# Decay attention and a sticky mixture of experts: batch 0's queries and keys turned by TensorE, its loads reordered, gates that count their transfer, a two-column minimum in one view, and less room for four ranked experts

## The chip, the cores and the metric

The kernel runs on one core of a Trainium2 chip. The metric is the device time in microseconds, as the median of several executions. Fewer is better.

## The reference

```python
scores = scale * q @ k^T                           # 8 batches, 8 heads, 576 positions, head size 64, scale 1/8
cum    = cumsum(log(clip(f, 1e-4, 1)))
attn   = softmax(causal(scores + cum[:, None] - cum[None, :]))
x      = (attn @ v) as [8, 576, 512]               # the heads side by side
logits = x @ w_gate; local = sigmoid(x @ w_local)  # 8 experts
for each batch, for s in order:                    # the routing is sticky
    e = argmax(logits[s]) if s == 0 or local[s] < 0.5 else prev_e
    out[s] = softmax(logits[s])[e] * (relu(x[s] @ w1[e]) @ w2[e])   # w1 512x1024, w2 1024x512
```

The inputs are fp32 and drawn at random.

## The kernel before

**Attention, batch by batch.** fp32 values are split into a high and a low fp16 part. For every batch the queries and keys are turned so that head size lies on partitions: tile A holds high and low parts on 128 partitions, tile B (`QB`, `KB`) the high part on 64 partitions and six rows more that carry the decay. A score is two products, A by A and B by B. A batch has 25 units: for each pair of heads a c, two a, a b and a c unit, then four d units for the last 64 positions and one more. Each unit passes through stages: scores on TensorE (`sc`, L868), row maximum on VectorE (`mx`, L879), exponential on ScalarE (`ex`, L899), the transposition of the weights on TensorE (`tr`, L914), the split on ScalarE and VectorE (`hi`, L919, `lo`, L923), the product with v on TensorE (`av`, L893), and the division by the sum (L954, L958). In d units the maximum is the smaller of two negated maxima (`mn`, L986).

**What sets the order.** The engines' queues are written by hand. A planner (`issue`, `start_of`, `step`) keeps a clock for each engine with estimated costs, and issues next the stage that could start first, with weights. A list `DUE` of times on that clock triggers groups of moves (`moves`, lists `ORD0`, `ORDA`, `ORDB`): loads, splits on GpSimd, turning. All transfers but indirect ones stand in the SyncE queue, which issues strictly in order and waits at each until its source is ready and its destination free. From batch 2 on, queries and keys are turned in groups of eight blocks by TensorE (`prep_turned`, `group`, stages `tq` and `eq`); a `needs` entry keeps scores behind them. From batch 1 on, the load buffer of one batch is refilled with the next one's as soon as it has been split.

**Batch 0, before.** `start` lets ScalarE (`high`) and GpSimd and VectorE (`low`) split queries and keys of heads 0 to 3 into fp16. TensorE turns these heads (`turn_high`, L552, `turn_first`, L546), adds the decay rows by a small product (`add_decay`, L557), and ScalarE and VectorE copy the results out of PSUM (`untwist`). Heads 4 to 7 and the last positions are turned by transfers (`turn`, `turn_last`) and copied by more transfers. The values are split by ScalarE and VectorE for heads 0 to 5 (`due_v`, `split_v`). The decay's parts for the last 64 positions, `spt`, are made on VectorE (`parts`, L247 and L251) in `start`.

**Gate and routing.** When a batch's attention is done, its rows are split on GpSimd and turned by three transfers (`finish_main`, `finish_last`). A side chain then runs the gate (`mult`, L816) of that batch on TensorE, with a routing step (`route`) for every second batch. `side_next` tells when the next piece of the chain may run: before, a gate may be issued once its three transfers have been issued.

**Experts.** The first two experts have fixed places, the other six are sorted by their number of tokens. Each rank has room for a fixed number of tokens (`CAP2`, `RANK2`, in units of 64). `experts` computes z = x w1 (L1690, 192 products of half the room's columns, or 96 of all of them up to 512) and y = h w2 (L1712, 24 products of 512 columns for every 128 tokens; a last 64 tokens take 48 products of 256 columns, L1716). Tokens above the room go to a loop at the end, one round of 128 tokens each, which does not run when there are none.

```python
after.append(ends[dep])                          # start_of: a stage waits for the one before it
if due and due[0][0] <= t and all(room[r] for r in due[0][2]):
    due.popleft()[1]()                           # issue: moves that have come due go first
```

## Time and profile before

| | |
|---|---|
| median of 3 runs | 856.01 us (855.11 to 859.09) |
| the profiled execution, its own time | 858.83 us |
| its span, first to last instruction | 857.1 us |
| TensorE busy | 785.4 us, 92% |
| VectorE, ScalarE, GpSimd busy | 529.3, 434.4, 408.9 us |
| granted TensorE clock, mean | 0.976 |
| moved by DMA | 122.46 MB, 143 GB/s |

The span minus the busy time of the engine that bounds is what waits cost at most. Attention ends at about 440 us; the experts fill the rest. Rows of merged instructions give one start and the whole length, and a product's length contains its passage through the array, so the rate of a stream of products is read from starts.

### The profile page before, as it was taken

To read this page: it belongs to the slowest core of one execution; us is meant where nothing else is said; L and a number is where in the kernel's file an instruction comes from. 1 tells how busy PE (TensorE), PEld (TensorE's weight loads), DVE (VectorE), ACT (ScalarE), POOL (GpSimd) and SP (SyncE) were. 2 spreads that over 40 slices of the span, in tenths; PEclk is the share of its full clock that TensorE was granted. 3 is DMA by queue.
4 is the path that set the end of the run, shared out by engine and by line. 5 is a ranking of instruction groups with operands and counts; after the bars stand their busy time and mean duration, and the time that the engine had idled before them with its cause. 6 is when DMAs were issued, how large, how long until landed. Compare 5 with 4: busy or idle time off the path is not lost. (4 is left out here: it accounts for less than half of the span.)

```text
span 857.1 us, 21126 instructions
## 1 busy us (share of the span) xinstructions
PE 785.4 (92%) x8510; PEld 546.9 (64%) x8510; DVE 529.3 (62%) x1125; ACT 434.4 (51%) x807; POOL 408.9 (48%) x479
## 2 busy tenths in 40 slices
PE   5897999889998799878987899999999999999996
PEld 3676778767877678767753555575564847566543
DVE  8885878898867888798848742443163644525120
ACT  4785878758866688657821413333242423324221
POOL 9598938488753968532976252221311212130201
PEclk9998999999989999998999999999999999999999
DMA  7979768596781859329674641848264553736101
GB/s 167 192 165 193 160 112 168 123 180 144 140 197 42 157 140 158 70 47 229 161 165 185 194 142 50 216 147 203 95 171 149 155 182 121 193 116 185 51 0 47
DMA packets 196517, 122.46 MB, mean 143 GB/s; under 512 B 136220, under 2 KB 172318, under 8 KB 196396
## 3 DMA queue, kind: packets, MB, share of 16 engines
q1 hardware_dynamic: 190273, 101.68, 51.6%
...
## 5 line engine op out<-in xcount | busy, mean ns | idle before, releaser
L1690 PE MATMUL z<-xT,wh 128*128 128x288 f16 (+4 forms) x960 | 182.3, 301 | 3.8 <-DVE hl L1671 3.8
L899 ACT ACTIVATE P<-st,nm 128x512 f32<-128x512 f32 (+3 forms) x288 | 152.4, 584 | 38.5 <-DVE nm L879 35.3
L879 DVE TENSOR_REDUCE nm<-st 128x1 f32<-128x512 f32 (+4 forms) x264 | 134.1, 542 | 23.2 <-PE st L875 16.8
L1671 DVE SCALAR_TENSOR_TENSOR hl<-z,hh 128x576 f16<-128x576 f32 (+5 forms) x80 | 53.0, 662 | 154.0 <-ACT hh L1670 153.8
L919 ACT CAST ph<-pt 128x512 f16<-128x512 f32 (+1 forms) x200 | 115.8, 583 | 50.1 <-PE pt L914 48.6
L914 PE MATMUL pt<-ident,P 128*128 128x128 f32 x784 | 124.7, 283 | 13.0 <-DVE pl L923 8.0
L923 DVE TENSOR_TENSOR pl<-pt,ph 128x512 f16<-128x512 f32 x168 | 111.6, 668 | 26.3 <-ACT ph L919 24.0
L1690 PEld LDWEIGHTS <-wh 128*128 128x128 f16 x960 | 93.2, 98 | 43.7 <-issue 4.9
L1690 PE MATMUL z<-xT,wl 128*128 128x288 f16 (+4 forms) x480 | 118.4, 301 | 0.0
L1712 PE MATMUL y<-uh,hh 128*128 128x512 f16 x288 | 109.9, 381 | 1.6 <-ACT o L1680 1.6
L1712 PE MATMUL y<-uh,hl 128*128 128x512 f16 x288 | 109.9, 382 | 0.0
L1712 PE MATMUL y<-ul,hh 128*128 128x512 f16 x288 | 109.7, 381 | 0.0
L1670 ACT ACTIVATE hh<-z 128x576 f16<-128x576 f32 (+5 forms) x80 | 46.0, 575 | 121.1 <-PE z L1690 121.0
L914 PEld LDWEIGHTS pt<-ident,P 128*128 128x128 f32 x784 | 85.8, 144 | 28.9 <-issue 7.5
L1712 PEld LDWEIGHTS <-hh 128*128 128x128 f16 x576 | 56.5, 98 | 70.4 <-issue 6.2
L1682 POOL DMA_INDIRECT out_dram<-o,ranki x26 | 27.3, 1051 | 149.0 <-ACT o L1680 115.8
L893 PE MATMUL xp<-VH,pl 128*128 128x65 f16 (+1 forms) x960 | 92.3, 195 | 4.3 <-DVE pl L923 4.3
L893 PE MATMUL xp<-VH,ph 128*128 128x65 f16 (+1 forms) x960 | 94.3, 198 | 0.9 <-ACT ph L919 0.9
L893 PE MATMUL xp<-VL,ph 128*128 128x65 f16 (+1 forms) x960 | 93.2, 196 | 0.0
L893 PEld LDWEIGHTS <-ph 128*128 128x128 f16 (+1 forms) x1920 | 85.0, 103 | 7.7 <-issue 2.5
L868 PE MATMUL st<-KB,QB 70*128 70x256 f16 (+4 forms) x448 | 80.1, 287 | 8.5 <-DMA KB<-Ak 7.1
L868 PE MATMUL st<-Ak,Aq 128*128 128x256 f16 (+4 forms) x448 | 80.7, 291 | 7.3 <-ACT P L899 7.1
...
## 6 DMA issues: line engine op xcount, KB each, us to landing
...
```

Of the source, the lines that this page charges most:

```text
L868: nc.tensor.matmul(st[p0:p0 + m, co:co + n], lhsT=queries(lq, kk, h, c), rhs=rhs, start=(ps == 0 and first and co == col), stop=(ps == 1), ...
L879: nc.vector.tensor_reduce(dst, src, axis=AX.X, op=ALU.max, negate=True)
L893: nc.tensor.matmul(xo, lhsT=a[:, c0:c0 + m], rhs=w[:, vi, :], start=False, stop=(i == n - 1 and jj == 2), skip_group_check=True)
L899: nc.scalar.activation(P[:, c0:c1].rearrange("p (k x r) -> p k r x", r=2, x=64), st[:, c0:c1].rearrange("p (k r x) -> p k r x", r=2, x=64) ...
L914: nc.tensor.matmul(U["pt"][:, i * 128:(i + 1) * 128], lhsT=P[:, i * 128:(i + 1) * 128], rhs=ident, is_transpose=True, start=(i == 0), stop ...
L919: nc.scalar.copy(U["ph"][:, :cols], U["pt"][:, :cols])
L923: nc.vector.tensor_tensor(U["pl"][:, :cols], U["pt"][:, :cols], U["ph"][:, :cols], ALU.subtract)
L1670: nc.scalar.activation(hv, z[:, 0:nh, 0:wd], AF.Relu)
L1671: nc.vector.scalar_tensor_tensor(lv, z[:, 0:nh, 0:wd], 0.0, hv, ALU.max, ALU.subtract)
L1682: nc.gpsimd.indirect_dma_start(out=outf, out_offset=bass.IndirectOffsetOnAxis(ap=scat(t), axis=0), in_=o, in_offset=None, bounds_check=NT ...
L1690: nc.tensor.matmul(z[:, a, 0:wd], lhsT=w[:, d, fc * 128:(fc + 1) * 128], rhs=xT[:, x, a * wd:(a + 1) * wd], start=(i == 0), stop=(i == len ...
L1712: nc.tensor.matmul(y, lhsT=a[:, fc, t * 128:(t + 1) * 128], rhs=u[:, fc], start=(i == 0), stop=(i == len(prods) - 1))
```

## The change

Experts' rooms are now given in tokens: 608, 608, 576, 576, 544 and 480 for the six ranks, where they were 640, 640, 576, 576, 576 and 512. The two fixed experts keep 640 and 704. Parts of tiles of 96 and 32 tokens take the place of whole and half tiles.

In batch 0, TensorE transposes fp32 queries and keys of heads 0 to 3 as they were loaded (`turn_head`), ScalarE takes the high part out of PSUM and a second time with the decay rows (`head_hi`, `head_b`), and VectorE the low part (`head_lo`). Heads 0 and 1 are turned ahead of the decay, head 2 right behind it, head 3 as a planned stage (`head_3`). Heads 4 to 7 and the last positions become planned groups like those of later batches (`group`, `first_turns`), and the transposing transfers of batch 0 are gone. GpSimd no longer scales queries, splits the values of heads 2 to 7, and makes `spt` (`last_parts`). Fills of `QB` and `spk` go from GpSimd to ScalarE and VectorE. `ORD0` is now three lists at three due times; the loads of batch 2's queries and keys leave `ORDB` and get due times of their own (`ORDC`). A gate's start on the planner's clock has to lie 4500 ns behind the estimated end of its batch's last split (`XR`, `XL`). `mn` is a reduction over two columns of one strided view. Batch 0's units 10 to 24 get `needs`.

```diff
-CAP2 = (10, 11)
-RANK2 = (10, 10, 9, 9, 9, 8)
+CAPC = (640, 704)
+RANKC = (608, 608, 576, 576, 544, 480)
...
-ORD0 = moves_of("q:l :k2 q:t4 k:l q:p k:t4 q0:m :sv k:p q:c k:c q1:m q:t k:t :lm q:M k:m :at 0:R 1:R :lv")
+ORD0 = moves_of("k:A q:A q:l k:l :k2 :sv q:p k:p")
+ORD1 = moves_of('q0:m q1:m')
+ORD2 = moves_of(':lm q:M k:m k:M :sp :at 0:R 1:R :lv q:a k:a')
...
-DUE = (("k2", 11000), ("q2", 12500), ("k3", 14500), ("q3", 15500), ("v", 18000), ("v4", 20500), ("a", 26000), ("b", 29000))
+XL = 4500
+LATE = ((12500, 'kh'), (13500, 'qh'), (15500, 'q2'), (15500, 'q3'), (17500, 'k2'), (17500, 'k3'), (22000, 'q4'), (23000, 'k4'))
+DUE = (('k2', 11500), ('q2', 12300), ('0', 12500), ('1', 20600), ('2', 25000), ('a', 27000), ('b', 29000), ('c0', 47000), ('c1', 56000))
...
-    for c in range(2):
-        nc.gpsimd.memset(QB[0][64:70, 16 * c + 8:16 * c + 16], -1.0)
...
+    spk = cp.tile([97, 512], F16, name="spk")
+    nc.vector.memset(spk, 0.0)
+    nc.vector.memset(spk[96:97], 1.0)
     nc.vector.memset(KB[0][64:70, 16:32], 1.0)
-
-    spk = cp.tile([97, 512], F16, name="spk")
-    nc.gpsimd.memset(spk, 0.0)
-    nc.gpsimd.memset(spk[96:97], 1.0)
+    for c in range(2):
+        nc.scalar.activation(flat(QB[0][64:70, 16 * c + 8:16 * c + 16]), ident[64:70, 0:1].broadcast_to([6, 1024]), AF.Copy,
+                             scale=0.0, bias=-1.0)
...
+    for t, x in (pick[:, 0, :, 3:6], 1.0 / SCALE), (pick[:, 1, :, 0:3], 1.0):
+        nc.gpsimd.affine_select(out=t, in_=t, pattern=[[-1, 4], [-32, 3]], compare_op=ALU.not_equal, fill=x, base=0,
...
+    def group(b, nm, j):
...
+        def tq():
+            t16 = Tq[b][nm + "t"]
+            U["pt"] = psS.tile([128, 8, 128], F16, name="st")
+            for a in range(4 if j == 4 else 8):
+                nc.tensor.transpose(U["pt"][:, a], t16[:, 8 * j + a], ident16)
...
+        return {"key": (b, nm, j), "tq": ("PE", 460 * c, tq, {"psS": 1}, {}), "eq": (eng, cost, eq, {}, {"psS": 1})}
...
+    def last_parts():
+        x = cu[:, 512:576]
+        for j in range(3):
+            nc.gpsimd.tensor_scalar(spt[:, j], x, 1.0, 1.0, ALU.mult, ALU.mult)
+            if j < 2:
+                nc.gpsimd.tensor_tensor(x, x, spt[:, j], ALU.subtract)
...
+    def turn_head(h, nm):
+
+        st = psX.tile([128, 512], F32, name="xp") if h == 2 else psS.tile([128, 512], F32, name="st")
         for a in range(4):
-            nc.tensor.transpose(pt[:, a], Tq[0][nm + "t"][:, 4 * h + a], ident16)
-        return pt
-
-    def turn_high(h, nm):
-        st, c0 = psS.tile([128, 512], F32, name="st"), 64 * (nm == "k")
-        for a in range(4):
-            nc.tensor.matmul(st[0:64, 128 * a:128 * a + 128], lhsT=Tq[0][nm + "t"][:, 4 * h + a, c0:c0 + 64], rhs=ident16,
+            nc.tensor.matmul(st[0:64, 128 * a:128 * a + 128], lhsT=LT[0, nm][:, 4 * h + a], rhs=ident, is_transpose=True,
                              start=(a == 0), stop=True, skip_group_check=True)
         return st
...
+    def head_hi(st, h, nm):
+        nc.scalar.activation(of_head(Tq[0][nm + "A"], TOP if nm == "q" else LOW, h, nm), of_bank(st, 64, nm), AF.Copy,
+                             scale=SCALE if nm == "q" else 1.0)
+
+    def head_b(st, h, nm):
+        nc.scalar.activation(of_head(Tq[0][nm + "B"], slice(0, 70), h, nm), of_bank(st, 70, nm), AF.Copy,
+                             scale=SCALE if nm == "q" else 1.0)
+
+    def head_lo(st, h, nm):
+        A = Tq[0][nm + "A"]
+        hi = of_head(A, TOP if nm == "q" else LOW, h, nm)
+        if nm == "q":
+            for c in range(2):
+                dst, src, top = (x[:, :, c] for x in (of_head(A, LOW, h, nm), of_bank(st, 64, nm), hi))
+                nc.vector.scalar_tensor_tensor(dst, src, SCALE, top, ALU.mult, ALU.subtract)
         else:
-            copy(by_head(dst, n, h), pt[0:n].rearrange("p (a c x) -> p a c x", a=4, c=2) if len(pt.shape) == 2 else
-                 pt.rearrange("p a (c x) -> p a c x", c=2))
+            nc.vector.tensor_tensor(of_head(A, TOP, h, nm), of_bank(st, 64, nm), hi, ALU.subtract)
...
-        high("q", 0, 2, True)
-        high("k", 0, 2)
-        high("k", 2, 4)
-        high("q", 2, 4)
         other_masks()
-        for h in range(2):
-            low("q", h, h + 1, nc.gpsimd, True)
-            low("k", h, h + 1, nc.gpsimd)
-        low("k", 2, 4, nc.gpsimd)
+        for C in range(2):
+            load_main(0, "q", C, 4, 8)
         load_v(0, groups=((0, 2),), last=False)
+        for C in range(2):
+            load_main(0, "k", C, 4, 8)
         by_chunks()
         parts(spm, lg[:, 0:512], 1, True)
-        for C in range(2):
-            load_main(0, "q", C, 4, 8)
         put_aug()
-        heads(0)
-        low("q", 2, 4, nc.vector)
-        heads(1)
-        parts(spt, cu[:, 512:576], 0)
-        split_v(0, 2, True)
-        for C in range(2):
-            load_main(0, "k", C, 4, 8)
+        for h in range(2):
+            heads(h)
+            for nm in "kq":
+                head_hi(HS[h, nm], h, nm)
+        decays(0)
+        decays(1)
+        heads(2)
+        decays(2)
+        for h in range(2):
+            for nm in "kq":
+                head_b(HS[h, nm], h, nm)
+                head_lo(HS[h, nm], h, nm)
         load_v(0, groups=((2, 8),), last=False)
-        for nm in "kq":
-            aug_main(0, nm, 4)
-
-        for nm in "qk":
-            for x in pieces(nm, 4, 8):
-                x()
+        vh, vl, v0 = parts_v(0, 2)
+        nc.scalar.copy(vh, v0)
+        for x in pieces("q", 4, 8):
+            x()
+        nc.gpsimd.tensor_tensor(vl, v0, vh, ALU.subtract)
+        for x in pieces("k", 4, 8):
+            x()
+        split_v(2, 4)
+
+    def due_0():
         for nm in "qk":
             LT[1, nm] = LT[0, nm]
             new_prep(1, nm)
         for x in ORD0:
+            moves(x)
+
+    def due_1():
+        assert all(n > -9 or u['key'][2] > 1 for n, u, _ in line['tq'])
+        for x in ORD1:
+            moves(x)
+
+    def due_2():
+        for x in ORD2:
...
+    def due_head(nm):
+        head_hi(HS[2, nm], 2, nm)
+        head_b(HS[2, nm], 2, nm)
+        head_lo(HS[2, nm], 2, nm)
+        clock["ACT"] += 960
+        clock["DVE"] = max(clock["DVE"] + 640, clock["ACT"] + 800)
+
+    def head_3(nm):
+        U = {}
+
+        def tq():
+            U["st"] = turn_head(3, nm)
+            add_decay(U["st"], 3, nm)
+
+        def eq():
+            for f in head_hi, head_b, head_lo:
+                f(U["st"], 3, nm)
+            clock["DVE"] = max(clock["DVE"], clock["ACT"] + 1100) + 640
+
+        return {"key": (0, nm, -1), "tq": ("PE", 500, tq, {"psS": 1}, {}), "eq": ("ACT", 960, eq, {}, {"psS": 1})}
+
+    def first_turns():
+        for t, x in LATE:
+            u = head_3(x[0]) if x[1] == "h" else group(0, x[0], int(x[1]))
+            u["ready"] = t
+            n = count[0] * 1e-4 - 10
+            count[0] += 1
+            for st, prev in ("tq", None), ("eq", "tq"):
+                line[st].append((n, u, prev))
...
+            XR[b] = max(clock["POOL"], clock["PE"]) + XL
...
-                nc.vector.tensor_tensor(nm[:, c:c + 1], nm[:, 44:45], nm[:, 40 + j:41 + j], ALU.min)
+                nc.vector.tensor_reduce(nm[:, c:c + 1], nm[:, 40 + j:45:4 - j], axis=AX.X, op=ALU.min)
...
-        for i, u in enumerate(units if b > 1 else ()):
-            u["needs"] = [(b, x, min(i // 10 * 2 + 1, 4) if i < 20 else 4) for x in "qk"]
+        for i, u in enumerate(units):
+            u["needs"] = [(b, x, min(i // 10 * 2 + 1, 4) if i < 20 else 4) for x in "qk"] if b > 1 or b == 0 and i > 9 else ()
...
-    clock = {"PE": T0, "ACT": T0, "DVE": T0, "POOL": T0}
+    clock = {"PE": T0, "ACT": T0 + 900, "DVE": T0 + 1300, "POOL": T0}
...
+        if hasattr(chain[0], "batch") and side["run"] is None:
+            after.append((XR[chain[0].batch], "PE"))
...
-        nt = 128 * n + (64 if half else 0)
+        n, mh = (nt // 128, nt % 128) if half else ((nt + 127) // 128, 0)
...
+                    m = min(128, nt - 128 * t)
+                    nc.tensor.matmul(y[0:m], lhsT=a[:, fc, t * 128:t * 128 + m], rhs=u[:, fc], start=(i == 0),
...
+                        nc.tensor.matmul(y[mh * r:mh * r + mh, 0:DM // 2], lhsT=a[:, fc, t * 128:t * 128 + mh],
```

**SyncE queue, batch 1's turned queries and keys against batch 2's loads** (ldq and ldk are the load buffers of queries and keys, Aq, Ak, QB and KB the tiles A and B). Before:

```order
L182 DMA ldv<-in_v_dram 128x8x64
L185 DMA ldv<-in_v_dram 64x4x64 x2
L162 DMA ldq<-in_q_dram 128x8x128 x2
L169 DMA ldq<-in_q_dram 64x4x64 x2
L162 DMA ldk<-in_k_dram 128x8x128 x2
L169 DMA ldk<-in_k_dram 64x4x64 x2
L378 DMA QB_121<-Aq 64x2x1024 x2
L382 DMA QB_121<-Aq 64x512
L375 DMA KB_123<-Ak 64x2048 x2
L382 DMA KB_123<-Ak 64x512
```

Now:

```order
L182 DMA ldv<-in_v_dram 128x8x64 x2
L185 DMA ldv<-in_v_dram 64x4x64 x2
L362 DMA QB_109<-Aq 64x2x1024 x2
L366 DMA QB_109<-Aq 64x512
L162 DMA ldq<-in_q_dram 128x8x128 x2
L169 DMA ldq<-in_q_dram 64x4x64 x2
L359 DMA KB_111<-Ak 64x2048 x2
L366 DMA KB_111<-Ak 64x512
L162 DMA ldk<-in_k_dram 128x8x128 x2
L169 DMA ldk<-in_k_dram 64x4x64 x2
```

Each pair of copies of batch 1 now stands ahead of batch 2's load of the same tensor; before, both loads stood ahead of all copies.

**SyncE queue, the late tokens of batch 3** (xl, turned into xlt for the gate; xr are the other tokens). Before:

```order
L341 DMA QB_121<-augm 3x32x64 x2
L351 DMA QB_121<-augt 3x512
L757 DMA xs<-xr 64x4x1024 x2
L378 DMA QB_121<-Aq 64x2x1024 x2
L382 DMA QB_121<-Aq 64x512
L339 DMA KB_123<-augm 3x4096
L351 DMA KB_123<-augt 3x512
L781 DMA_TRANSPOSE xlt<-xl 128x4x128
L787 DMA xs<-xl 128x1x256 x2
```

Now:

```order
L343 DMA QB_109<-augm 3x32x64 x2
L353 DMA QB_109<-augt 3x512
L732 DMA xs<-xr 64x4x1024 x2
L756 DMA_TRANSPOSE xlt<-xl 128x4x128
L763 DMA xs<-xl 128x1x256 x2
L362 DMA QB_109<-Aq 64x2x1024 x2
L366 DMA QB_109<-Aq 64x512
```

The transfer that turns xl stood behind the copies of batch 4's queries, and stands ahead of them now.

**VectorE at the start of batch 7** (HI, RH and LO are the marks of a routing step, nm the row maxima, pl the low parts of the weights). Before:

```order
L1473 TENSOR_TENSOR hm<-t_192,ov 128x10
L1479 TENSOR_TENSOR HI<-imain,hm 128x480
L1483 TENSOR_SCALAR RH<-HI,irow 128x10x48
L1485 TENSOR_SCALAR RH<-HI,irow 128x2x48
L1490 TENSOR_TENSOR RH<-HI,icol 128x10x48
L1491 TENSOR_TENSOR LO<-i_176,lo 128x1280
L879 TENSOR_REDUCE nm<-st 128x1 x5
L879 TENSOR_REDUCE nm<-st 128x2
L879 TENSOR_REDUCE nm<-st 128x1
L1501 TENSOR_TENSOR invi<-st,invi 128x96
```

Now:

```order
L1451 TENSOR_TENSOR hm<-t_188,ov 128x10
L855 TENSOR_REDUCE nm<-st 128x1 x2
L1457 TENSOR_TENSOR HI<-imain,hm 128x480
L855 TENSOR_REDUCE nm<-st 128x2
L1461 TENSOR_SCALAR RH<-HI,irow 128x10x48
L899 TENSOR_TENSOR pl<-pt,ph 128x512
L1463 TENSOR_SCALAR RH<-HI,irow 128x2x48
L855 TENSOR_REDUCE nm<-st 128x1
L1468 TENSOR_TENSOR RH<-HI,icol 128x10x48
L1469 TENSOR_TENSOR LO<-i_172,lo 128x1280
L930 RECIPROCAL rs<-xp 128x4
L899 TENSOR_TENSOR pl<-pt,ph 128x512
```

The five marks stood together ahead of the maxima, and are now spread between maxima and splits.

## Rows read from the trace of the kernel before

**Rows 1.** Busy time in stretches of the span: the stretch and its length, then for PE, PEld, DVE, ACT and POOL the busy microseconds (and the instructions), PEclk (the TensorE clock that was granted: 1.00 is 2.4 GHz, 0.50 is 1.2 GHz), the share of the DMA engines, and GB/s.
```profile
72.00:76.00 4.00, 1.20 (x7) 0.83 (x7) 0.47 (x1) 0.00 (x0) 3.92 (x5) 0.58 1.18 165
76.00:80.00 4.00, 4.00 (x68) 3.33 (x66) 2.42 (x6) 2.44 (x5) 1.97 (x2) 0.57 0.84 60
...
248.00:252.00 4.00, 4.00 (x24) 2.80 (x23) 1.74 (x6) 2.33 (x4) 0.00 (x0) 0.50 0.93 252
...
352.00:356.00 4.00, 4.00 (x33) 2.91 (x32) 3.09 (x10) 2.00 (x5) 3.71 (x6) 0.57 0.08 18
...
388.00:392.00 4.00, 4.00 (x23) 3.00 (x23) 2.60 (x5) 2.40 (x6) 0.00 (x0) 0.50 1.09 255
392.00:396.00 4.00, 4.00 (x45) 2.98 (x43) 3.26 (x12) 2.81 (x6) 0.74 (x1) 0.81 0.96 311
680.00:700.00 20.00, 19.85 (x124) 11.75 (x122) 12.63 (x17) 7.23 (x10) 4.36 (x3) 1.00 0.75 205
```

**Rows 2.** Timeline of TensorE in the first microseconds: start, length, engine, line and operation, out<-in, shapes, and how many instructions were merged into the row; in brackets the idle time ahead of it and what ended that.
```profile
12.13 1.01 PE L557 MATMUL st<-spk,pick 97*6 97x512 f16 x2 [0.74 <-DVE spk L246]
...
15.98 0.61 PE L868 MATMUL st<-Ak,Aq 128*128 128x512 f16 x1
...
16.91 0.63 PE L868 MATMUL st<-Ak,Aq 128*128 128x128 f16 x3
...
17.98 0.41 PE L868 MATMUL st<-Ak,Aq 128*128 128x128 f16 x3
...
24.28 0.38 PE L546 MATMUL pt<-ident,t16k 128*128 128x128 f16 x4 [2.17 <-DVE Ak L561]
...
26.93 1.06 PE L914 MATMUL pt<-ident,P 128*128 128x128 f32 x4
```

**Rows 3.** Timeline of VectorE there, same columns. L247 and L251 make the fp16 parts of the decay (spm the first 512 positions, spt the last 64), L879 is a row maximum.
```profile
9.10 0.42 DVE L247 CAST spm<-lg 64x512 f16<-64x512 f32 x1
...
15.48 1.05 DVE L247 CAST spt<-cu 64x64 f16<-64x64 f32 x1
...
16.82 2.00 DVE L247 CAST spt<-cu 64x64 f16<-64x64 f32 x1
...
19.88 3.14 DVE L247 CAST spt<-cu 64x64 f16<-64x64 f32 x1
...
22.56 1.34 DVE L879 TENSOR_REDUCE nm<-st 128x1 f32<-128x512 f32 x3
```

**Rows 4.** Timeline of ScalarE there, same columns: the logarithm, the table load for the exponential, one head's copy out of PSUM, the first exponential.
```profile
5.01 0.68 ACT L229 ACTIVATE lg<-ft 64x576 f32<-64x576 f32 x1 [2.93 <-DVE ft L228]
5.71 1.28 ACT L230 ACT_TABLE_LOAD   x1
...
12.75 0.58 ACT L561 CAST KB<-st 70x512 f16<-70x512 f32 x1 [2.81 <-PE st L557]
...
23.27 0.71 ACT L899 ACTIVATE P<-st,nm 128x512 f32<-128x512 f32 x1 [1.90 <-DVE nm L879]
```

**Rows 5.** Timeline of GpSimd: the first split of batch 1's queries.
```profile
38.67 1.05 POOL L310 TENSOR_SCALAR t16q<-ldq 128x1024 f16<-128x1024 f32 x1 [6.08 <-DMA ldq<-in_q_dram]
```

**Rows 6.** Timeline of the SyncE queue; a length here is the time to issue, x the number of transfers. The first load of batch 2 (three more like it follow), and the copies of batch 1's key halves.
```profile
56.62 1.59 SPq L162 DMA_DIRECT2D ldq<-in_q_dram  x2
...
66.67 2.68 SPq L375 DMA_DIRECT2D KB<-Ak  x2
```

**Rows 7.** Timeline of TensorE where batch 1 begins.
```profile
69.89 0.38 PE L868 MATMUL st<-Ak,Aq 128*128 128x512 f16 x1
74.80 0.59 PE L868 MATMUL st<-KB,QB 70*128 70x512 f16 x1 [4.53 <-DMA KB<-Ak]
```

**Rows 8.** Timeline of GpSimd in the gate of batch 3: the last split of its late tokens (xl).
```profile
237.41 0.67 POOL L314 TENSOR_TENSOR xl<-xnl,xl 128x256 f16<-128x256 f32 x1
```

**Rows 9.** Timeline of the SyncE queue there: batch 4's copies of query halves, then the transfer that turns xl.
```profile
239.91 1.76 SPq L378 DMA_DIRECT2D QB<-Aq  x2
...
243.77 1.83 SPq L781 DMA_TRANSPOSE xlt<-xl  x1
```

**Rows 10.** Timeline of TensorE there.
```profile
246.74 0.59 PE L816 MATMUL st<-wg,xlt 128*64 128x18 f16 x8 [1.94 <-DMA xlt<-xl]
```

**Rows 11.** Who TensorE waited for, over the whole span: line, microseconds in total, times, longest.
```profile
PE st L816 <- DMA xlt<-xl: 4.4, 2, 2.4
...
PE st L868 <- DMA KB<-augt: 1.4, 1, 1.4
```

**Rows 12.** Timeline of VectorE as batch 7 begins: the first of five marks of a routing step, and the row maxima behind them.
```profile
380.89 1.46 DVE L1479 TENSOR_TENSOR HI<-imain,hm 128x480 f16<-128x480 f16 x1
...
386.45 3.32 DVE L879 TENSOR_REDUCE nm<-st 128x1 f32<-128x512 f32 x7
```

**Rows 13.** Timeline of TensorE there.
```profile
387.92 0.59 PE L868 MATMUL st<-Ak,Aq 128*128 128x512 f16 x1 [4.66 <-ACT P L899]
```

**Rows 14.** Timeline of TensorE in the experts: two products that follow each other.
```profile
452.37 0.38 PE L1712 MATMUL y<-uh,hh 128*128 128x512 f16 x1
452.58 0.38 PE L1712 MATMUL y<-ul,hh 128*128 128x512 f16 x1
```

**Rows 15.** VectorE's groups by shape: count, busy microseconds, mean ns, idle time ahead.
```profile
L986 DVE TENSOR_TENSOR nm<-nm 128x1 f32<-128x1 f32 x32 | 8.6, 269 | 1.0
...
L954 DVE RECIPROCAL rs<-xp 128x2 f32<-128x2 f32 x32 | 5.1, 160 | 2.6 <-PE xp L893 1.9
```

More of the change, by code (lines that the diff above doesn't have):

```diff
@@ L693, in due_b @@
     def due_b():
+        assert all(n > -9 for n, u, _ in line['tq'])
         for x in ORDB:
@@ L696, in due_b, with due_c @@
         open_small()
+        EX["run"] = True
+    def due_c(i):
+        for x in ORDC[i]:
+            moves(x)
     def pieces(nm, h0, h1):
@@ L730, in split_v, with decays @@
-    def split_v(h0, h1, fast=False):
-        tv = [x.rearrange("p (c h) d -> p c h d", c=4) for x in (VH[0][:, 0:32], VL[0][:, 0:32], LT[0, "v"][:, 0:32])]
-        split(tv[0][:, :, h0:h1, 0:64], tv[1][:, :, h0:h1, 0:64], tv[2][:, :, h0:h1], fast)
-    def due_v(h0, h1):
-        split_v(h0, h1, True)
-        clock["ACT"] += 480
-        clock["DVE"] += 600
-    XT, XD = {}, {}
+        for nm in "kq":
+            HS[h, nm] = turn_head(h, nm)
+    def decays(h):
+        for nm in "kq":
+            add_decay(HS[h, nm], h, nm)
@@ L1636, in early_weights, with tokens @@
         return out
-    def tokens(pool, xT, cols, n, rows=NT, half=False):
-        for i in range(n + half):
-            m = 128 if i < n else 64
+    def tokens(pool, xT, cols, n, rows=NT):
+        for i in range((n + 127) // 128):
+            m = min(128, n - 128 * i)
             xg = pool.tile([128, 2 * DM], F16, name="xg", bufs=3)
@@ L1773 @@
                 init_gate()
-            if not due:
+            if "run" in EX:
                 if b < B - 1 or i < XP:
```

291 lines of the change are left out of this document (104 added, 187 removed).

## The prediction

> **What bounds the kernel now.** The windows come first: in the experts TensorE is busy 19.85 of 20 us at full clock [rows 1], so time is saved there only by giving it fewer columns. Attention is different. It ends at about 440 us, and TensorE waits in a few places for a transfer or an exponential; after such a wait the granted clock was 0.50 to 0.58, that is 1.2 GHz for all or most of 4 us, with TensorE busy all or most of them [rows 1], so a wait costs its length and about 2 us more. The timelines of the engines, TensorE first and then the one that it waited for, give the places; the list of waits gives the totals. The profiled execution took 858.83 us, 2.8 above the median of 856.01, and the sum is made against it. A measurement of this kernel can tell 0.5%, 4.3 us, from no change.
>
> **a. Batch 0's start.** Before, the two decay products run at 12.13 and the first score at 15.98 [rows 2]. Its maximum comes only at 22.56 [rows 3] and the exponential at 23.27 [rows 4]: ahead of it VectorE makes `spt`, three casts of 64 columns that take 1.05, 2.00 and 3.14 us, where a cast of 512 columns took 0.42 [rows 3]. TensorE waits 2.17 us and transposes the first weights at 26.93 [rows 2].
>
> Now ScalarE first fills `QB` (two instructions; with the table load of 1.28 [rows 4] that is 3.3 us by a length of 1.0 each, my choice between the 0.58 of a copy [rows 4] and the 1.76 us of VectorE's fill of twice the columns that falls away, so 1 is near the middle), against 2.93 us that it was idle ahead of the logarithm [rows 4]: the decays come 0.4 later. TensorE then runs four decays ahead of the scores, and head 2's eight transposes. Two decays took 1.01 with their passage through the array, so four take about 1.7; four fp32 transposes took 1.06 [rows 2], so head 2's eight about 1.7. With 0.9 for ScalarE's copies, which the scores wait for, the first score starts at 12.5 + 1.7 + 1.7 + 0.9 = 16.8, 0.8 later. But `spt` is on GpSimd and not in front of the maxima: with maximum and exponential following as they did ahead of the transposes, those stand at 20 to 21.7 instead of 26.93, with one more unit scored by then (0.5). Still to be done after that are head 3 (1.3) and the 40 transposes of the groups, 2.2 at 0.054 each (128 columns at the rate in f). Net: 26.93 - 21.7 + 0.5 - 1.3 - 2.2 = 1.25 with the late end and 2.95 with the early one; the 1.0 us in which ScalarE waited [rows 4] for copies that now need no VectorE adds up to 1.0 to both. I take **-3.1** of 1.25 to 3.95, near the top, since no `spt` is left ahead of the first maximum. ScalarE gets about 3.1 us more of copies there, at nothing, beside its idle 2.81 and 1.90 [rows 4]; without that cover they cost 3.1. GpSimd waits 6.08 us for batch 1's load [rows 5], so its `spt` and splits have room; if it is late, groups q4 and k4 are, by about 1 us.
>
> The new transposes weigh on the clock. The same three score products took 0.63 at 16.91 and 0.41 at 17.98 [rows 2]: the clock rose from half to full while TensorE did transposes, decays and scores in turn. The Trainium skill, "TensorE: Matmul & The Clock Gate", section "Part 4: PE-mode transpose", says that full clock does not engage for transpose mode, which is not counted as busy in the same way. By it the start gives +0.9 and not -3.1. Of what TensorE did ahead of the rise only a part were transposes, so the trace does not refute it; it is rival C.
>
> **b. Batch 1's halves.** The queue issues batch 2's load at 56.62, waits for its buffer, and reaches the copy of key halves at 66.67 [rows 6]. TensorE does the first product at 69.89 and waits 4.53 us for that copy [rows 7]; the clock is 0.58 and 0.57 behind it [rows 1], and 0.43 of the 5.2 us up to 80 is 2.2 lost. Now both copies stand ahead of the loads they waited behind. The load itself leaves later, at due times of its own, and has 50 us until batch 2. I take **-6.8** of 0 to -6.8.
>
> **c. The gates.** GpSimd has split the late tokens at 238.1 [rows 8], but the transfer that turns them goes out at 243.77 [rows 9], behind batch 4's copies. The gate waits 1.94 [rows 10]; two gates wait 4.4 in all [rows 11], with the clock at 0.50 and 0.57 behind them [rows 1]: 2.0 + 1.7. Now the transfer stands ahead of these copies, and the gate is planned 4500 ns behind the split. Behind a waiting gate stood scores, and behind SyncE's transfer batch 4's halves, which go 1.8 later but are not yet needed. **-8.1** of 0 to -8.1.
>
> **d. The last decay rows of batch 0** stood behind batch 1's in SyncE's queue, and are put ahead of them (ORD2). The wait for KB<-augt, 1.4 [rows 11], goes: **-1.4**; late next would be KB's last copy, which stands directly behind.
>
> **e. Marks of a routing step.** VectorE does five of them in one go from 380.89, maxima pile up to seven at 386.45 [rows 12], and TensorE waits 4.66 for an exponential [rows 13]; the clock is 0.50, then 0.81 [rows 1], 2.0 + 0.8 more: 7.5. Now maxima stand between the marks. But no rule makes it so; it fell out of a plan that differs from batch 0 on. Half: **-3.7** of 0 to -7.5.
>
> **f. The experts' rooms.** z takes 192 products of half the room: 16 columns fewer for 608 against 640, twice, 2 x 3072; 544 against 576 is the same 3072; 480 against 512 is 96 products by 32 columns, 3072. y keeps its columns: a part tile of 96 tokens still moves 512, one of 32 still 48 times 256. Products follow each other 0.21 us per 512 columns [rows 14], 0.42 ns each: 12288 columns are **-5.2**, the surest term, since nothing else bounds there.
>
> **g. The minimum.** 32 of them took 269 ns; the nearest row of an instruction on two columns is the reciprocal, 160 ns [rows 15]. 0 to -3.5; only d units wait for it, and I take **-1.0**. The Trainium skill, "VectorE: DVE Perf Modes", section "Rules for kernel authors", speaks against it: it calls a reduction the slowest operation of VectorE. By it this term would be 0 or a small plus; no row of before has a reduction of two columns.
>
> **h. The other plan.** Every stage from batch 0 on is issued in another order. A new wait can cost from 0 to what the largest cost here, 7.5. The trace has five large ones in eight batches, of which I have taken four to go and one half; one that comes back nearly whole is likely: **+6**, between 0 and 15 (two whole ones).
>
> Sum: -3.1 - 6.8 - 8.1 - 1.4 - 3.7 - 5.2 - 1.0 + 6 = -23.3, so 835.5 on this execution and about **835** for the median.
>
> **Rivals.** A: the plan gives back all that c and e save, 11.8 in place of h's 6. For: nothing in the list of moves fixes where marks fall. Against: the order of the two excerpts of SyncE's queue is fixed. 835 + 5.8 = 841. Chance 0.21.
> B: the change does not do what it says in batch 1: the copies stand ahead of the loads, but their source, the turned groups, is planned as late as before. +6.8: 842. Chance 0.08.
> C: the fp32 transposes leave the clock at half through batch 0. Two stretches of 4 us, as 76 to 80 [rows 1], cost 2 each: the start gives +0.9 and not -3.1, 839. For: these scores begin at half clock. Against: they show it rise [rows 2]. Chance 0.12. The section of the Trainium skill named in a has it so.
> D: slower. A rank's tokens are more than its smaller room, and the loop at the end runs. One round loads an expert's weights, 4.19 MB, at 205 GB/s [rows 1] 20.5 us, and does 96 products of 128 columns and 24 of 512, 5.2 + 5.2: 31 us on 835, at least 866. It decides from one token above the room. Counted from the reference on inputs of its own kind, the six ranks hold 600, 580, 570, 556, 516 and 470 tokens for 608, 608, 576, 576, 544 and 480: new margins of 8 and more, but the inputs need not be mine. Chance 0.04.
>
> **How the numbers follow.** The forecast has 0.55. Low end: all terms at their best, without h: 858.8 - 3.9 - 6.8 - 8.1 - 1.4 - 7.5 - 5.2 - 3.5 = 822, so 823. High end: A and B together, and the 1.4 of d lost: 849, so 850; D is left out. Below 851.7 lie the forecast, A, B and C: 0.96 less 0.04 for several new waits together, which would end within 0.5%. Faster 0.92, same 0.04, slower 0.04.
>
> **What would show it.** First score near 16.8 and first transposes of weights near 21 (before, 26.93); no wait for KB in batch 1 at about 70 and clock 1.00 behind it; no gate that waits over 0.5 us for xlt; no row of seven maxima ahead of batch 7; the experts' TensorE busy time 5 us less; `mn` under 269 ns. The forecast is wrong if attention ends less than 10 us earlier than before, if a clock of 0.5 stands anywhere new for more than 8 us, or if the loop at the end runs.

## The result and the profile after

| | before | changed |
|---|---|---|
| median | 856.55 us (4 runs) | 832.88 us (829.01 to 834.57, 4 runs) |
| ratio, 95% interval | | 0.9715 (0.9677 to 0.9753) |
| the profiled execution, and its span | 858.83, 857.1 | 832.94, 831.2 |
| TensorE busy, mean granted clock | 785.4, 0.976 | 771.2, 0.988 |

The forecast was 835, in a range of 823 to 850. The profiled executions differ by 25.9 us.

Where they came from is read from one mark per batch: the small product (1x4) that begins the last units of a batch on TensorE. The first two of the changed kernel:

```profile
63.47 0.17 PE L859 MATMUL xp<-eps 1*128 1x4 bf16 x1
...
112.70 0.17 PE L859 MATMUL xp<-eps 1*128 1x4 bf16 x1
```

So batch 0 takes 63.5 and batch 1 takes 112.70 - 63.47 = 49.2. In the same way for all kernels below (us; "rest" is from the last mark to the end of the span):

| kernel | 0 | 1 | 2 | 3 | 4 | 5 | 6 | 7 | rest |
|---|---|---|---|---|---|---|---|---|---|
| before | 67.2 | 54.0 | 44.1 | 54.0 | 50.1 | 54.8 | 51.5 | 51.3 | 430.2 |
| **changed** | 63.5 | 49.2 | 44.9 | 48.1 | 49.6 | 53.9 | 48.3 | 46.8 | 426.9 |
| changed, old rooms | 62.6 | 48.2 | 44.9 | 48.1 | 48.1 | 55.0 | 48.3 | 47.5 | 431.8 |
| changed, spt on VectorE | 67.1 | 53.3 | 44.9 | 49.4 | 48.1 | 55.2 | 48.3 | 47.0 | 426.0 |
| changed, loads early | 61.9 | 56.5 | 44.9 | 48.1 | 49.5 | 54.0 | 48.4 | 47.4 | 427.0 |
| changed, no gate delay | 62.0 | 48.2 | 47.9 | 53.2 | 48.3 | 53.4 | 53.0 | 51.4 | 426.0 |
| changed, other weights | 62.7 | 45.0 | 44.4 | 60.2 | 45.2 | 60.3 | 44.9 | 50.8 | 425.1 |
| before, gate delay | 68.5 | 54.6 | 44.1 | 53.9 | 45.7 | 50.0 | 47.9 | 52.0 | 432.0 |
| before, copies first | 68.8 | 48.0 | 48.0 | 54.7 | 48.6 | 54.0 | 51.5 | 51.7 | 432.2 |
| changed, delay 6500 | 60.7 | 48.7 | 45.1 | 47.2 | 46.1 | 51.0 | 46.1 | 50.3 | 424.2 |
| changed, minimum of two operands | 60.6 | 48.7 | 44.9 | 48.1 | 49.6 | 55.9 | 48.3 | 49.2 | 423.5 |
| changed, more transposes | 64.3 | 48.2 | 44.9 | 49.3 | 48.1 | 55.5 | 48.3 | 45.8 | 430.1 |
| changed, split later | 62.3 | 48.2 | 44.9 | 49.3 | 48.0 | 55.2 | 48.3 | 46.0 | 427.6 |
| before, spt on GpSimd | 68.3 | 54.9 | 44.1 | 53.8 | 48.8 | 53.7 | 51.5 | 52.8 | 428.3 |

Each row is one execution. Where a run keeps the changed kernel's order of instructions in a stage, batch 0 took 60.6 to 63.5, batch 1 48.2 to 49.2, batch 3 48.1 to 49.4, batch 6 48.3 or 48.4, batch 7 45.8 to 49.2, so single entries are good to about 2 us. The change gained 3.7 in batch 0, 4.8 in batch 1, 5.9 in batch 3, 3.2 in batch 6, 4.5 in batch 7 and 3.3 behind them, and little elsewhere.

**The start.** TensorE of the changed kernel (columns as in [rows 2]): four decays, a transposed head, the first score, the first transposes of weights.

```profile
11.82 1.38 PE L483 MATMUL st<-spk,pick 97*6 97x512 f16 x4 [2.76 <-DVE spk L248]
13.13 1.06 PE L478 MATMUL xp<-ident,ldk 128*64 128x128 f32 x4
...
15.88 0.39 PE L844 MATMUL st<-Ak,Aq 128*128 128x512 f16 x1
...
18.93 0.61 PE L890 MATMUL pt<-ident,P 128*128 128x128 f32 x4
```

VectorE there: a cast of the decay, then the first maximum, 5.6 us earlier than in [rows 3].

```profile
11.70 2.23 DVE L249 CAST spm<-lg 64x512 f16<-64x512 f32 x1
...
16.93 0.69 DVE L855 TENSOR_REDUCE nm<-st 128x1 f32<-128x512 f32 x1
```

Windows of the changed kernel (columns as in [rows 1]): about half clock (0.59, 0.56) while the decays and head 2 are turned, full clock from the first score on, and half clock again behind the waits for the first weights.

```profile
12.00:14.00 2.00, 2.00 (x9) 0.90 (x8) 1.97 (x2) 1.77 (x4) 1.65 (x1) 0.59 0.07 17
14.00:16.00 2.00, 2.00 (x8) 0.72 (x7) 1.96 (x4) 1.19 (x3) 1.14 (x2) 0.56 0.32 70
16.00:18.00 2.00, 2.00 (x25) 1.68 (x24) 1.91 (x5) 1.12 (x3) 1.92 (x2) 1.00 1.02 217
...
22.00:24.00 2.00, 2.00 (x12) 1.46 (x10) 1.33 (x3) 1.80 (x4) 1.98 (x3) 0.65 0.13 30
24.00:26.00 2.00, 2.00 (x9) 1.14 (x8) 1.37 (x2) 0.73 (x2) 1.77 (x5) 0.50 0.27 51
```

**Batch 1.** The wait of 4.53 [rows 7] is 1.12 now, and the product behind it has the length of full clock (0.38; 0.59 in [rows 7]):

```profile
69.92 0.38 PE L844 MATMUL st<-KB,QB 70*128 70x512 f16 x1 [1.12 <-DMA KB<-Ak]
```

**The gate of batch 3.** In SyncE's queue the transfer that turns xl goes out ahead of the copies, and TensorE waits for nothing ([rows 9, 10] before):

```profile
223.53 4.61 SPq L756 DMA_TRANSPOSE xlt<-xl  x1
...
229.53 1.34 SPq L362 DMA_DIRECT2D QB<-Aq  x2
```

```profile
229.94 0.95 PE L792 MATMUL st<-wg,xt 128*128 128x18 f16 x32
230.82 0.42 PE L792 MATMUL st<-wg,xlt 128*64 128x18 f16 x8
```

**Marks at batch 7.** Maxima stand between them, where [rows 12] had five in one go:

```profile
364.21 0.64 DVE L1457 TENSOR_TENSOR HI<-imain,hm 128x480 f16<-128x480 f16 x1
364.77 0.68 DVE L855 TENSOR_REDUCE nm<-st 128x2 f32<-128x512 f32 x1
365.38 0.33 DVE L1461 TENSOR_SCALAR RH<-HI,irow 128x480 f16<-128x480 f16 x1
```

**What TensorE waits for.** No line for xlt or KB<-augt is left ([rows 11] before). Exponentials hold scores 0.7 at most (before 4.66, [rows 13]). Largest now are VectorE's low parts of the weights, 16.3 in 20 waits, and a wait of 2.3 in the last routing step is new:

```profile
PE pt L890 <- DVE pl L899: 11.6, 14, 1.9
...
PE xp L869 <- DVE pl L899: 4.7, 6, 2.3
...
PE st L844 <- ACT P L875: 3.5, 9, 0.7
...
PE psG L1475 <- DVE LOl L1469: 2.3, 1, 2.3
```

Before, the low parts held TensorE for 12.3 in 19 waits:

```profile
PE pt L914 <- DVE pl L923: 8.0, 14, 1.8
...
PE xp L893 <- DVE pl L923: 4.3, 5, 1.3
```

### The profile page after: what moved, and what is told of

Its sections match the earlier page's. It is cut to its first block, busy times and chain, and to the rows that moved or that the text cites. A ratio compares the mean times of both kernels' runs of the same rounds, so it can differ in the third digit from the quotient of the medians.

```text
span 831.2 us, 21136 instructions
## 1 busy us (share of the span) xinstructions
PE 771.2 (93%) x8518; PEld 544.2 (65%) x8518; DVE 522.8 (63%) x1130; ACT 438.6 (53%) x814; POOL 403.7 (49%) x478
## 5 line engine op out<-in xcount | busy, mean ns | idle before, releaser
L1669 PE MATMUL z<-xT,wh 128*128 128x304 f16 (+6 forms) x960 | 178.8, 298 | 3.8 <-DVE hl L1649 3.8
L1649 DVE SCALAR_TENSOR_TENSOR hl<-z,hh 128x384 f16<-128x384 f32 (+6 forms) x80 | 51.9, 649 | 147.0 <-ACT hh L1648 146.9
L1669 PE MATMUL z<-xT,wl 128*128 128x304 f16 (+6 forms) x480 | 116.6, 297 | 0.0
L1693 PE MATMUL y<-uh,hh 128*128 128x512 f16 (+1 forms) x288 | 109.7, 381 | 2.5 <-ACT o L1659 2.5
L1693 PE MATMUL y<-ul,hh 128*128 128x512 f16 (+1 forms) x288 | 109.5, 380 | 0.0
L1693 PE MATMUL y<-uh,hl 128*128 128x512 f16 (+1 forms) x288 | 109.4, 380 | 0.0
L1648 ACT ACTIVATE hh<-z 128x384 f16<-128x384 f32 (+6 forms) x80 | 45.2, 564 | 116.0 <-PE z L1669 115.9
L1693 PEld LDWEIGHTS <-hh 128*128 128x128 f16 (+1 forms) x576 | 57.5, 100 | 69.7 <-issue 6.2
L844 PE MATMUL st<-Ak,Aq 128*128 128x256 f16 (+4 forms) x448 | 77.0, 282 | 3.5 <-ACT P L875 3.5
L869 PEld LDWEIGHTS <-pl 128*128 128x128 f16 (+1 forms) x960 | 75.5, 103 | 5.7 <-DVE pl L899 5.4
```

What stands on the lines that cost most here:

```text
L844: nc.tensor.matmul(st[p0:p0 + m, co:co + n], lhsT=queries(lq, kk, h, c), rhs=rhs, start=(ps == 0 and first and co == col), stop=(ps == 1), ...
L869: nc.tensor.matmul(xo, lhsT=a[:, c0:c0 + m], rhs=w[:, vi, :], start=False, stop=(i == n - 1 and jj == 2), skip_group_check=True)
L1648: nc.scalar.activation(hv, z[:, 0:nh, 0:wd], AF.Relu)
L1649: nc.vector.scalar_tensor_tensor(lv, z[:, 0:nh, 0:wd], 0.0, hv, ALU.max, ALU.subtract)
L1669: nc.tensor.matmul(z[:, a, 0:wd], lhsT=w[:, d, fc * 128:(fc + 1) * 128], rhs=xT[:, x, a * wd:(a + 1) * wd], start=(i == 0), stop=(i == len ...
L1693: nc.tensor.matmul(y[0:m], lhsT=a[:, fc, t * 128:t * 128 + m], rhs=u[:, fc], start=(i == 0), stop=(i == len(prods) - 1))
```

## Experiments

| kernel | median us | ratio to before, 95% interval |
|---|---|---|
| changed | 832.88 | 0.9715 (0.9677 to 0.9753) |
| changed, old rooms | 835.59 | 0.9756 (0.9731 to 0.9781) |
| changed, minimum of two operands | 831.39 | 0.9717 (0.9683 to 0.9751) |
| changed, spt on VectorE | 837.88 | 0.9767 (0.9742 to 0.9791) |
| changed, loads early | 839.54 | 0.9805 (0.9776 to 0.9834) |
| changed, no gate delay | 846.81 | 0.9891 (0.9854 to 0.9929) |
| changed, other weights | 842.02 | 0.9854 (0.9825 to 0.9883) |
| changed, more transposes | 832.07 | 0.9684 (0.9652 to 0.9716) |
| changed, split later | 831.54 | 0.9696 (0.9668 to 0.9725) |
| changed, delay 6500 | 827.97 | 0.9648 (0.9619 to 0.9677) |
| before, gate delay | 850.39 | 0.9935 (0.9913 to 0.9957) |
| before, spt on GpSimd | 857.68 | 1.0004 (0.9988 to 1.0020) |
| before, copies first | 857.30 | 0.9997 (0.9979 to 1.0015) |

### The old rooms

```diff
-RANKC = (608, 608, 576, 576, 544, 480)
+RANKC = (640, 640, 576, 576, 576, 512)
```

> The changed kernel with the old rooms for the six ranked experts (640, 640, 576, 576, 576, 512) and nothing else different. My theory (term f): +5.2 us against the changed kernel's 832.9, so about 838, since the experts' stage is bound by TensorE's columns: 12288 columns at 0.42 ns. Rival: the stage is partly set by waits for VectorE (marks, splits) that fall beside, since from the end of attention to the end of the program the changed kernel was only about 3.2 us shorter: then +3 or less, 836.

+2.7 by medians, with intervals that overlap; the rest of the program is 431.8 for 426.9, +4.9. TensorE's z products by groups (count, busy, mean) in this kernel, and in the changed one:

```profile
L1669 PE MATMUL z<-xT,wh 128*128 128x288 f16 (+4 forms) x960 | 182.3, 301 | 3.8 <-DVE hl L1649 3.8
...
L1669 PE MATMUL z<-xT,wl 128*128 128x288 f16 (+4 forms) x480 | 118.4, 301 | 0.0
```

```profile
L1669 PE MATMUL z<-xT,wh 128*128 128x304 f16 (+6 forms) x960 | 178.8, 298 | 3.8 <-DVE hl L1649 3.8
...
L1669 PE MATMUL z<-xT,wl 128*128 128x304 f16 (+6 forms) x480 | 116.6, 297 | 0.0
```

300.7 less 295.4 is 5.3: the columns were worth what term f says. How much of it reached the end, one pair of runs does not tell. In the table above the rest is 428.3 to 432.2 in the five rows with the old rooms and 423.5 to 430.1 in the nine with the new; the means are 4.6 apart, so most of it did.

### The minimum of two operands

```diff
-nc.vector.tensor_reduce(nm[:, c:c + 1], nm[:, 40 + j:45:4 - j], axis=AX.X, op=ALU.min)
+nc.vector.tensor_tensor(nm[:, c:c + 1], nm[:, 44:45], nm[:, 40 + j:41 + j], ALU.min)
```

> The changed kernel with the minimum of two columns as a tensor_tensor again, same order on every engine. In the trace the 32 instructions took 152 ns each instead of 269. Theory (term g): d units wait for it in part, +1.0 of at most 3.7 us, 834. Rival 1: all of it is on the path, +3.7, 836.6. Rival 2: VectorE has slack there, 0, 832.9.

No difference. One line's instructions, shortest, median and longest in ns, here and in the changed kernel:

```profile
L962 DVE TENSOR_TENSOR nm<-nm x32: 134/160/1434, 55.1 to 399.8; 128x1 f32<-128x1 f32 x32
```

```profile
L962 DVE TENSOR_REDUCE nm<-nm x32: 128/155/157, 58.0 to 399.4; 128x1 f32<-128x2 f32 x32
```

The usual instruction is as long as it was. Of those with two operands ten took over 0.25 us, and each of them ended within 0.03 us of the end of an instruction of GpSimd. Of the reductions 16 began while GpSimd worked, and none took over 157 ns. But the total did not move, so nothing that sets the end waited for them.

### spt on VectorE

```diff
                 head_lo(HS[h, nm], h, nm)
+        parts(spt, cu[:, 512:576], 0)
...
-            last_parts()
```

> The changed kernel with spt made on VectorE in front of the first row maxima, as before, and not on GpSimd; the order of all else is the same. Theory (term a): this is the larger part of the start's gain. The three casts and two subtractions last 4 to 7 us beside GpSimd's splits, the first maximum moves from 16.9 to 21 or later, and the end by +3 to +5 us: 836 to 838. Rival: the start is bound by the transposes and ScalarE's copies, and the wait is made up within batch 0: 0 to +1.

+5.0: 3.7 in batch 0 and 4.1 in batch 1, the latter a copy of keys that is late again (a wait of 2.78). VectorE and GpSimd there:

```profile
17.27 2.13 DVE L253 TENSOR_TENSOR cu<-cu,spt 64x64 f32<-64x64 f32 x1
...
20.02 0.68 DVE L856 TENSOR_REDUCE nm<-st 128x1 f32<-128x512 f32 x1
```

```profile
17.20 2.12 POOL L666 TENSOR_TENSOR t16k<-ldk,t16k 128x1024 f16<-128x1024 f32 x1
```

The small subtraction begins with GpSimd's large one (17.20 to 19.32) and ends with it (19.40); the next, alone, took 0.22.

### spt on GpSimd in the kernel before

```diff
-        parts(spt, cu[:, 512:576], 0)
...
+            for j in range(3):
+                nc.gpsimd.tensor_scalar(spt[:, j], x, 1.0, 1.0, ALU.mult, ALU.mult)
+                if j < 2:
+                    nc.gpsimd.tensor_tensor(x, x, spt[:, j], ALU.subtract)
             nc.sync.dma_start(out=augt.rearrange("j p t -> p j t"), in_=spt)
```

> The kernel before with spt made on GpSimd (at the due time at which it is stored) and not on VectorE ahead of the first maxima; the order of all else is the same. Theory (term a): the start is shortened by this alone; putting spt back into the changed kernel cost 5 us, so -3 to -5 us, 852 to 854, with the first maximum at about 16.5 us. Rival: before, the transposes and copies of heads 2 and 3 stood between anyway, so that it pays only together with the new turning: 0 to -1, 856.

Nothing, though TensorE transposes the first weights at 23.63 instead of 26.93. The time comes back where heads 4 to 7 are first needed: TensorE, and the copy that it waits for in SyncE's queue, behind the transposing transfers of these heads.

```profile
37.31 0.59 PE L872 MATMUL st<-KB,QB 70*128 70x512 f16 x1 [4.91 <-DMA KB<-Ak]
```

```profile
20.98 3.44 SPq L365 DMA_TRANSPOSE Aq<-t16q  x2
...
31.19 0.52 SPq L375 DMA_DIRECT2D KB<-Ak  x1
```

So the start's gain has two halves that are worth nothing apart: maxima that start early (batch 0 took 68.3 here), and all the rest of the new start, with heads 4 to 7 that no transfer turns (67.1 in the changed kernel with spt on VectorE). The kernel before took 67.2. Which part of that second half is needed was not tried.

### Loads early, and copies first

The changed kernel with batch 2's loads ahead of batch 1's copies again, and the kernel before with copies ahead of loads; in both only SyncE's queue differs.

```diff
-('c0', 47000), ('c1', 56000)
+('c0', 29500), ('c1', 29600)
```

```diff
-ORDB = moves_of("... 3:V q:G1 k:G0 :vl :Vl q:2 k:G1 :iv v0:P k:2")
+ORDB = moves_of("... 3:V q:G1 k:G0 :vl :Vl k:G1 :iv v0:P")
+ORDC = moves_of("q:2"), moves_of("k:2")
-DUE = (..., ("b", 29000))
+DUE = (..., ("b", 29000), ("c0", 53000), ("c1", 56000))
```

> The changed kernel with batch 2's loads of queries and keys put back ahead of all copies of batch 1's halves in SyncE's queue (their due times 29500 and 29600 instead of 47000 and 56000); nothing else moves. Theory (term b): the queue's order was the cause of the 4.5 us wait, so it comes back in part, with the clock at half behind it: +3 to +6 us, 836 to 839. Rival: the loads' buffers are now free earlier, because GpSimd splits batch 1's keys sooner (done at 54 us), so the queue gets past them in time: 0 to +1, 833.

> The kernel before with batch 2's loads of queries and keys issued behind batch 1's copies in SyncE's queue (due times of their own, 53000 and 56000); the order on all other engines is the same. Theory (term b): the wait of 4.5 us ahead of the second product of batch 1 goes, and the half clock behind it, 2.2: -4.5 to -6.8 against 857.0, 850 to 852.5. Rival: the copy's source is as late as the queue was (the keys' groups are turned just before 66), so only 1 to 2 us of the wait go: 855 to 856.

In the changed kernel +6.7, 7.3 in batch 1. TensorE, and the window behind the start of the wait:

```profile
72.73 0.58 PE L844 MATMUL st<-KB,QB 70*128 70x512 f16 x1 [5.54 <-DMA KB<-Ak]
```

```profile
72.00:76.00 4.00, 3.27 (x22) 2.53 (x22) 1.86 (x5) 1.32 (x3) 3.92 (x4) 0.50 0.76 104
```

In the kernel before the wait went too, and batch 1 is 6.0 shorter. But the total is the same, which neither expectation had: batch 2 is 3.9 longer, and the other 2 lie within the spread of the entries. GpSimd, idle for 10 us, begins to split batch 2's keys at 97.73, where it was 84.16 before: their load leaves at 91.26 (before, 60.32). The profile puts the idle time down to TensorE; with a load issued 6.5 us earlier I take the load for its cause, which is not shown apart. TensorE then waits for the keys' copy:

```profile
97.73 1.05 POOL L311 TENSOR_SCALAR t16k<-ldk 128x1024 f16<-128x1024 f32 x1 [9.98 <-PE pt L932]
```

```profile
120.78 0.38 PE L874 MATMUL st<-KB,QB 70*128 70x512 f16 x1 [2.21 <-DMA KB<-Ak]
```

The changed kernel begins that split at 83.35. There the loads come late enough for the copies and early enough for batch 2.

### The gate's delay

Taken out of the changed kernel, put alone into the kernel before, and set to 6500 ns.

```diff
-        if hasattr(chain[0], "batch") and side["run"] is None:
-            after.append((XR[chain[0].batch], "PE"))
```

```diff
+            XR[b] = max(clock["POOL"], clock["PE"]) + 4500
...
+        if hasattr(chain[0], "batch") and side["run"] is None:
+            after.append((XR[chain[0].batch], "PE"))
```

```diff
-XL = 4500
+XL = 6500
```

> The changed kernel without the delay that the planner gives to a gate (a gate may be issued when its three transfers have been issued, as before); the planner makes another order from batch 2 on. Theory 1 (term c, widened): the delay is what took away the waits for xlt, and since the planner then knows when the gate's results come, also waits of the routing steps behind it (batches 3, 4, 6 and 7 got 14.1 us shorter in the changed kernel): +6 to +14 us, 839 to 847, with a wait for xlt of over 1 us in the list. Rival: the waits went because the order fell otherwise from batch 0 on (term h), and the delay alone does nothing: 0 to +2, 833 to 835, no wait for xlt.

> The kernel before with the gate's delay of 4500 ns on the planner's clock and nothing else of the change. Theory 1 as for the run without it: -6 to -14 us against 856.8, 843 to 851. Rival: it is the plan from batch 0 on: within 2 us of 856.8.

> The changed kernel with a gate's delay of 6500 ns on the planner's clock instead of 4500. Theory: the delay works by being true, as a transfer takes that long to come; 2 us too much costs little by itself, no wait for xlt comes back, but it is another plan, so 833 to 842. Rival: any delay does, the plan's luck plays no part: 831 to 835.

Without it +13.9, and batches 3, 6 and 7 are as long as in the kernel before (53.2, 53.0, 51.4). What TensorE waits for, and then VectorE as batch 7 begins:

```profile
PE st L844 <- ACT P L875: 7.2, 6, 4.8
PE st L792 <- DMA xlt<-xl: 6.9, 3, 3.1
```

```profile
375.50 1.48 DVE L1467 TENSOR_TENSOR LO<-i,lo 128x1280 f16<-128x1280 f16 x1
376.90 3.32 DVE L855 TENSOR_REDUCE nm<-st 128x1 f32<-128x512 f32 x7
```

Both waits are back, and so is the row of seven maxima behind the marks. By its code the planner without the delay takes the gate's results to be there, and it places the routing steps that follow from them ahead of maxima. The run is another plan as well, so not all of the 13.9 need be the delay's.

In the kernel before the delay alone gives 6.6: 12.9 in batches 4 to 6 and nothing in 3 and 7 (the order of instructions is the same up to batch 4). No wait for xlt is left there, and the longest for an exponential is 1.7, though gates now wait 3.4 us for the other tokens. In SyncE's queue the transfer of xl still stands behind the copies, as in [rows 9]. The transfer is 1.8 later, as the whole batch is. What moved is the gate: it takes up the turned tokens at 253.82, where it waited for them until 246.74 [rows 10].

```profile
241.74 1.76 SPq L378 DMA_DIRECT2D QB<-Aq  x2
...
245.59 1.81 SPq L781 DMA_TRANSPOSE xlt<-xl  x1
```

```profile
253.82 0.42 PE L817 MATMUL st<-wg,xlt 128*64 128x18 f16 x8
```

So the order of the queue is not needed for this gate; to plan it later is enough.

With 6500 the changed kernel gains 4.9 more than with 4500, which neither expectation had: batches 4 to 6 are 8.6 shorter, batch 7 is 3.5 longer. By medians that version is faster than both kernels; its interval and that of the changed kernel touch at 0.9677. That a truer delay is the reason is not shown, since each value is another plan.

### Other weights

```diff
-W.update({'sc': -210, 'mx': -60,
+W.update({'sc': -200, 'mx': -70,
```

> The changed kernel with two of the planner's weights moved a little (scores -200 for -210, maxima -70 for -60), which means nothing by itself but gives another order of the same work from batch 0 on. It measures term h. Theory: another plan costs or gives up to one large wait, 7.5 us: within 825 to 841, and most likely slower, since the weights look chosen. Rival: plans of this planner differ by less than a measurement tells: 831 to 835.

+9.1. Batches 1, 4 and 6 are up to 4.4 shorter than in the changed kernel, but 3, 5 and 7 are 12.1, 6.4 and 4.0 longer. In 3 and 5 a routing step now waits for GpSimd:

```profile
PE st L1432 <- POOL EX L1425: 12.8, 2, 6.4
```

### More transposes

```diff
+        pt = psT.tile([128, 512], F32, name="pt")
+        for a in range(12):
+            nc.tensor.matmul(pt[:, 128 * (a % 4):128 * (a % 4) + 128], lhsT=ident, rhs=ident, is_transpose=True,
+                             start=True, stop=True, skip_group_check=True)
         decays(0)
```

> The changed kernel with 12 fp32 transposes of the identity more, in the gap of TensorE ahead of the decays (9.06 to 11.82 us), whose results nobody reads, so that TensorE does nothing but transposes from 5.5 to 11.8. Theory (rows): transposes count as work for the clock, so it is at full speed before the first score, the decays and head 2's transposes run faster (the eight in about 1.1 us and not 1.7), and the first score comes 0.5 to 1 us earlier than 15.88. Rival (the rule on transpose mode): the clock rises only with the decays and scores, the decays and head 2's transposes stay at 0.85 us for four, the first score at 15.9 or later. Total within 2 us of 832.9 in both.

TensorE, and a window:

```profile
8.93 2.35 PE L544 MATMUL pt<-ident 128*128 128x128 f32 x12
11.78 1.02 PE L483 MATMUL st<-spk,pick 97*6 97x512 f16 x4 [0.50 <-DVE spk L248]
12.73 0.63 PE L478 MATMUL xp<-ident,ldk 128*64 128x128 f32 x4
...
15.43 0.39 PE L848 MATMUL st<-Ak,Aq 128*128 128x512 f16 x1 [1.10 <-DVE Aq L509]
```

```profile
12.00:14.00 2.00, 2.00 (x14) 1.05 (x12) 1.97 (x2) 1.81 (x4) 1.61 (x1) 1.00 0.09 27
```

With nothing but transposes ahead of them, the decays (1.02 for 1.38) and head 2's transposes (0.63 for 1.06) run at full clock. Now VectorE's low parts are late, so the end does not move by more than the runs' spread.

### Split later

```diff
+        nc.gpsimd.tensor_tensor(vl, v0, vh, ALU.subtract)
         for x in pieces("q", 4, 8):
             x()
-        nc.gpsimd.tensor_tensor(vl, v0, vh, ALU.subtract)
```

> The changed kernel with two of GpSimd's pieces of work exchanged: the values' low part, which waits for ScalarE until 14.9, comes ahead of the split of queries 4 to 7 (10.35 to 13.65). All other queues are the same. Theory: VectorE's cast of spm from 11.70 (2.23 us, where the same cast at 9.01 took 0.42) was held until GpSimd's subtraction ended, so the cast falls to about 0.4, the low parts of heads 0 and 1 and the first maximum come 1.5 us earlier, and the end by 0 to 1.5: 831.4 to 833. Rival: the cast is slow for its own sake or for transfers: it stays at 2.2, the total goes up by the later groups, 833 to 835.

VectorE's cast, and then TensorE:

```profile
10.93 0.42 DVE L249 CAST spm<-lg 64x512 f16<-64x512 f32 x1
```

```profile
11.04 1.02 PE L483 MATMUL st<-spk,pick 97*6 97x512 f16 x4 [1.90 <-DVE spk L248]
...
14.24 0.61 PE L844 MATMUL st<-Ak,Aq 128*128 128x512 f16 x1
...
17.75 0.60 PE L890 MATMUL pt<-ident,P 128*128 128x128 f32 x4
```

With GpSimd idle, the same cast takes 0.42 instead of 2.23, and all that follows in the start is 1.2 to 1.6 earlier. The total is 1.3 lower, within the spread.

## Why the prediction was right, and where its steps were not

The sum was right (-23.3 forecast; -25.9 in the profiled executions, -23.7 by medians). The 835 for the median takes off less than the sum does: 856.01 less 23.3 is 832.7. Its terms were right in place, less so in size, and part of the agreement is luck:

- **a and d**, -4.5: batch 0 got 3.7 shorter, 4.5 to 6.6 in the other runs that leave it as it is. The sum of a is 1.0 off (its own numbers give 2.2 and 3.9 ahead of the 1.0, not 1.25 and 2.95), and VectorE's fill of 1.76 did not fall away; it stands at 2.34 in the changed kernel. The first score came at 15.88, not 16.8, and the weights at 18.93, below the forecast's 20. Of these 8.0 us the step itself gave 3.5 to head 3 and the groups; the waits of 0.6 and 1.1 behind the first weights and 1.7 lost by the clock from 22 to 26 it did not have. The step "spt is in front of the maxima" is right for the changed kernel (5.0 when put back) and wrong alone: before, the transposing transfers were next.
- **b**, -6.8: batch 1 got 4.8 shorter; 1.1 of the wait stayed. The order of the queue is the cause, as both runs show, but the start belongs to it: with spt on VectorE 2.78 of the wait is back. That the load "has 50 us until batch 2" holds for these due times and not for any.
- **c and e**, -11.8 together: the runs with and without the delay show both kinds of wait come and go together. Batches 4, 6 and 7, where they stood, gave 8.2. In c the step "the transfer stands ahead of these copies" is not needed: in the kernel before the delay takes the wait away with the old order of the queue. Whether that order helps by itself was not tried. In e the step "no rule makes it so", by which it was halved, failed: the gate's delay is that rule. It reaches batch 3 of the changed kernel as well, of which the prediction said nothing (5.9).
- **f**, -5.2: TensorE's z got 5.3 shorter, the rest of the program 3.3; new waits of the last routing step (2.3 for LOl) stand against it.
- **g**, -1.0: 0. The price of the instruction was no price of its work: it is the same in the median, and only some were held.
- **h**, +6: no large wait came back, as it had thought likely, but short ones did. TensorE waits 4.0 more for low parts and 2.3 for LOl. Batch 4 lost the gate's wait of 1.94 and the half clock of 2.0 and is only 0.5 shorter; TensorE idles 3.3 us in it, and 2.2 before. (Batch 2's +0.8 is no wait: TensorE idles 0.3 us in it, and 22 more products fall ahead of its mark.) Without h the terms add up to -29.3, and -25.9 was measured, so 3.4 of the 6 were wanted. That is what is left over of misses in both directions: a, d, b, f and g gave 5.7 less than their terms, c and e in their own batches 3.6 less, and batch 3 gave 5.9 that no term had. For another plan 9.1 was measured once, with other weights.

Of the rivals, A did not come and B came to a sixth (1.1 of 6.8). C is refuted: the clock is full from the first score on but for a stretch of 3 to 4 us, and the run with more transposes speaks against it. The loop of D did not run: z has 960 and 480 products in both kernels.
